# Half of k's features by wide VectorE operations at the start of an attention-and-mixer kernel

## The chip, the core and the metric

The kernel runs on one core of a Trainium2 chip. Its time is device time in microseconds (us), the median of several runs; lower is better. The core has a matrix engine (TensorE, PE in the profile), a vector engine (VectorE, DVE), a scalar engine (ScalarE, ACT), a general engine (GpSimd, POOL) and a queue engine (SyncE, SP) that issues most transfers. Each engine works through its own instructions in the order in which the program gave them; semaphores tie the engines together. The matrix engine writes its sums to PSUM; everything else here lies in SBUF, and inputs and output lie in device memory (HBM).

## What is computed

There are 8 batches, 8 heads, 576 positions and 64 features per head, all inputs float32.

```python
# linear attention with two position-weighted features of relu(q) and relu(k)
theta = pi/2 * pos / S
phi(x) = concat(relu(x) * cos(theta), relu(x) * sin(theta))     # 64 -> 128
kv  = sum over positions of phi(k)^T v          # 128 x 64 per head
z   = sum over positions of phi(k)
x   = (phi(q) kv) / (phi(q) z + 1e-6)           # heads side by side: 576 x 512
# mixer
u   = x + low-rank mix of x over positions (U: 576x32, V: 32x576)
out = u + relu(u @ w_ch1) @ w_ch2               # 512 -> 2048 -> 512
```

## The kernel before

**The bulk.** The mixer's two large products (`g1_main`, line 487, and `g2_part`, line 539) are 1,024 matrix instructions of 128x512, and they are the matrix engine's steady work. Batches go in pairs. The order of all work is written out by hand: a list of slots (one slot is one `g1_main` or a quarter of a `g2` row), and a table `todo` of what is emitted beside each slot. For batches 2 to 7 the attention of a batch is spread over the slots of the pair before it (`attention_plan`). For batches 0 and 1 there is no earlier work to hide behind: batch 0 is worked through by `chain0` before the first slot, and batch 1 is prepared beside slots 0 to 6 (`beside`, lines 754 to 766) and finished by `chain1` after slot 7.

**Batch 0.** Its chain is: load q, k and v; make phi(q) (`q_prep`), transpose it on the matrix engine (`qtr_unit`) and copy the result out of PSUM; make phi(k) (`k_prep`) and a bf16 copy of v with a column of ones (`v_prep`, tile `v_ext`); multiply the two (`kv_unit`); denominators (`den_unit`); x (`xh_unit`); and then the mixer's low-rank step down to the transposed u (`uT`), from which `g1_main` reads. k and v lie as four groups `g` of two heads, each with nine chunks `c` of 64 values per partition. `chain0` goes through the heads in two halves, groups 0 and 1, then groups 2 and 3.

**phi(k).** `k_prep(b, c, engs, g0, g1)` makes one chunk: one instruction for the cosine feature and one for the sine feature, each max(k, 0) times a per-partition weight (a [128, 1] column, since one chunk of one partition is one position). The pair `engs` names the engines. In batch 0's first half the cosine is on VectorE and the sine on ScalarE but for chunks 4 and 8; in its second half VectorE takes the cosine of four chunks and GpSimd that of five (line 659). GpSimd also makes `v_ext` of groups 2 and 3 (lines 661 and 662), after its five chunks. In batch 1 VectorE makes nine cosine chunks of 256 values and ScalarE nine sine chunks (line 760).

**Other pieces the change touches.** `V_four` spreads the small matrix V over PSUM and `V_evac` copies it to SBUF as `V_bf`, between the q transposes and phi(k). `keep_warm(n, tag, bufs)` issues n matrix instructions on zeros whose results nobody reads. SyncE's queue carries, in order: q, k and v of batch 0 in halves, with the tail of q (positions 512 to 575, tile `qt`) between them; then batch 1's q, k, tail of q, and v (lines 731 to 738). A tile with a single buffer can only be loaded when its last reader is done: the tail of q of batch 1 waits for `q_prep(0, 4, ...)`, and v of batch 1 for the four `v_prep` of batch 0. GpSimd issues the loads of `w_ch1` and `w_ch2` (tile `w_bf`), among its casts. The second quarter of `w_ch1` (`w1_load(1)`) comes right after `v_ext` of groups 2 and 3.

Of the kernel before, what the change touches and what calls it, by code (L numbers as in the profile page):

```python
# [13 lines left out]
ALU = mybir.AluOpType  # L14
# [3 lines left out]
def kernel(  # L18
# [11 lines left out]
    nc = tc.nc  # L30

    B = 8
    H = 8
    S = 576
    D = 64
    E = D + 1
    P = 128
# [13 lines left out]
    def tail(b):  # L51
        lo = TS * (b % 2)
        return slice(lo, lo + TS)
# [8 lines left out]
    kst, vst, qst, qt = {}, {}, {}, {}  # L62

    def alloc_k(b):
        kst[b] = pool.tile([P, 4, 9, D], FP32, tag="kst", bufs=2, name="kst")
# [4 lines left out]
    def load_nine(dst, src, b, g0=0, g1=4, eng=None):  # L70
        (eng or nc.sync).dma_start(
            out=dst[:, g0:g1, :, :].rearrange("p g c d -> p g (c d)"),
            in_=src[b].rearrange("(g hh) (p c) d -> (hh p) g (c d)", hh=2, c=9)[:, g0:g1, :],
        )
# [11 lines left out]
    def load_tail(dst, src, b, h0=0, h1=H, eng=None):  # L86
        (eng or nc.sync).dma_start(
            out=dst[tail(b), h0:h1, :],
            in_=src[b, h0:h1, 512:S, :].rearrange("h s d -> s h d"),
        )  # L90
# [4 lines left out]
    def w1_load(n):  # L95
        cs = slice(n * 512, n * 512 + 512)
        nc.gpsimd.dma_start(
            out=w1_bf[:, :, cs], in_=moe_w_ch1.rearrange("(d p) n -> p d n", p=P)[:, :, cs]
        )
# [7 lines left out]
    def cast(eng, o, i):  # L107
        if eng is nc.scalar:
            nc.scalar.activation(out=o, in_=i, func=AF.Copy, bias=0.0, scale=1.0)
        else:  # L110
            eng.tensor_copy(out=o, in_=i)  # L111


    V_, A_, G_ = nc.vector, nc.scalar, nc.gpsimd
# [6 lines left out]
        out=iota[:, 0:4], pattern=[[1, 4]], base=0, channel_multiplier=4,  # L121
        allow_small_or_imprecise_dtypes=True,
    )
    for lo in (0, TS):
        nc.gpsimd.iota(
            out=iota[lo : lo + TS, 4:5], pattern=[[1, 1]], base=512, channel_multiplier=1,
# [3 lines left out]
            out=iota[lo : lo + TS, 5:14], pattern=[[1, 9]], base=0, channel_multiplier=9,  # L130
# [13 lines left out]
    cosw = const.tile([P, 14], FP32)  # L144
    sinw = const.tile([P, 14], FP32)
# [21 lines left out]
        out=U_bf[:, 0:4, :], in_=moe_U[0:512, :].rearrange("(p c) r -> p c r", c=4)  # L167
# [12 lines left out]
    def keep_warm(n, tag, bufs):  # L180
        w_ps = ps.tile([P, 512], FP32, tag=tag, bufs=bufs, name="w_ps")
        for _ in range(n):
            nc.tensor.matmul(out=w_ps, lhsT=zero[:, 0:P], rhs=zero, start=True, stop=True)
# [6 lines left out]
    def V_four(tag, bufs):  # L190
        v4 = v4_ps[0] = ps.tile([P, 2, 512], FP32, tag=tag, bufs=bufs, name="v4_ps")
        lhs = four.rearrange("r g s -> r (g s)")
        nc.tensor.matmul(
            out=v4[:, 0, :].rearrange("m (c p) -> m c p", c=4), lhsT=lhs,
            rhs=V_32[:, 0:512].rearrange("r (p c) -> r c p", c=4), start=True, stop=True,
        )
        for i in range(2):
            nc.tensor.matmul(
                out=v4[:, 1, tail(i)], lhsT=lhs, rhs=V_32[:, 512:S], start=True, stop=True
            )  # L200

    def V_evac(eng):
        cast(
            eng, V_bf.rearrange("p c t -> p (c t)"),
            v4_ps[0].rearrange("p a n -> p (a n)")[:, 0 : 5 * P],
        )


    k_p, q_p, q_pT, kv_sb, x_bf, A_sb = {}, {}, {}, {}, {}, {}
    u_bf, u_tl, uT, uT_tl = {}, {}, {}, {}  # L210

    def v_prep(b, g, eng):
        cast(eng, v_ext[b % 2][:, g, :, 0:D], vst[b][:, g, :, :])
# [9 lines left out]
    def k_prep(b, c, engs, g0=0, g1=4):  # L223
        if b not in k_p:
            k_p[b] = pool.tile([P, 9, 4, 2 * D], BF16, tag="k_p", bufs=1, name="k_p")
        for i, (w, eng) in enumerate(zip((cosw, sinw), engs)):
            if eng is not None:
                scaled_relu(
                    eng, k_p[b][:, c, g0:g1, i * D : i * D + D], kst[b][:, g0:g1, c, :],
                    w[:, 5 + c : 6 + c],  # L230
                )

    def q_prep(b, c, engs, h0=0, h1=H):
        if b not in q_p:
# [10 lines left out]
    def kv_unit(b, g0=0, g1=4, eng=None):  # L245

        if b not in kv_sb:
            kv_sb[b] = pool.tile([P, H, E], BF16, tag="kv", bufs=2, name="kv")
        acc = ps.tile([P, 2, 512], FP32, tag="X", bufs=1, name="kv_ps")
        for g in range(g0, g1):  # L250
            for c in range(9):
                for hh in range(2):
                    rows = slice(hh * TS, hh * TS + TS)
                    nc.tensor.matmul(  # L254
                        out=acc[:, hh, (g - g0) * E : (g - g0) * E + E],
                        lhsT=k_p[b][rows, c, g, :],
                        rhs=v_ext[b % 2][rows, g, c, :],
                        start=(c == 0),
                        stop=(c == 8),
                    )  # L260
        cast(
            eng or V_,
            kv_sb[b][:, 2 * g0 : 2 * g1, :].rearrange("p (g hh) e -> p hh g e", hh=2),
            acc[:, :, 0 : (g1 - g0) * E].rearrange("p hh (g e) -> p hh g e", e=E),
        )
# [5 lines left out]
    def qtr_unit(b, c, h0=0, h1=H, eng=None, tag="T", bufs=1):  # L271
        qT_alloc(b)
        t_ps = ps.tile([P, H, P], BF16, tag=tag, bufs=bufs, name="t_ps")
        for h in range(h0, h1):
            nc.tensor.transpose(  # L275
                out=t_ps[:, h, :],
                in_=q_p[b][:, c, h, :] if c < 4 else q_tl[:, h, :],
                identity=ident,
            )
        if c < 4:  # L280
            cast(eng or V_, q_pT[b][:, c, h0:h1, :], t_ps[:, h0:h1, :])
        else:
            cast(eng or V_, q_tlT[:, h0:h1, tail(b)], t_ps[:, h0:h1, tail(b)])
# [14 lines left out]
    def qT_of(b, c, h):  # L298
        return q_pT[b][:, c, h, :] if c < 4 else q_tlT[:, h, :]
# [12 lines left out]
    def den_unit(b, h0, h1, tag, bufs):  # L312
        n = h1 - h0
        d_ps = ps.tile([P, 5, n], FP32, tag=tag, bufs=bufs, name="d_ps")
        for c in range(5):
            for h in range(h0, h1):
                nc.tensor.matmul(
                    out=d_ps[:, c, h - h0 : h - h0 + 1],
                    lhsT=qT_of(b, c, h),
                    rhs=kv_sb[b][:, h, D:E],  # L320
                    start=True,
                    stop=True,
                )
        rec = pool.tile([P, 5, n], FP32, tag="rec5", bufs=2, name="rec5")
        recip(rec, d_ps)
        return rec
# [312 lines left out]
    O2, G3 = ("o", 2), ("g", 3)  # L639
# [9 lines left out]
        uTd_open(b, 3, "o", 2)  # L649

    def chain0():
        v_prep(0, 0, V_)
        v_prep(0, 1, A_)
        q_prep(0, 4, (V_, A_))
        kv_unit(0, 0, 2)
        keep_warm(2, "o", 2)
        qtr_unit(0, 4, 0, H, V_, *G3)
        for c in range(9):
            k_prep(0, c, (V_ if c < 4 else G_, A_), 2, 4)
        rec0 = den_unit(0, 0, 4, "T", 1)  # L660
        for g in (2, 3):
            v_prep(0, g, G_)
        w1_load(1)
        for n, c in enumerate(TL):
            xh_unit(0, c, 0, 4, rec0, *(O2, O2, G3, G3, G3)[n], A_ if n == 1 else None)
        keep_warm(2, "T", 1)
        kv_unit(0, 2, 4, A_)
        rec1 = den_unit(0, 4, 8, "X", 1)
        a0 = A_unit(0, "T", 1, A_, 0, 256)
        for n, c in enumerate(TL[:3]):  # L670
            xh_unit(0, c, 4, 8, rec1, *(O2, O2, G3)[n])
        chain_begin(0)
        uTd_mm(0, 0)
        uTd_mm(0, 1)
        for n, c in enumerate(TL[3:]):
            xh_unit(0, c, 4, 8, rec1, *G3)
        uTd_evac(0, 0, A_)
        uTd_evac(0, 1, A_)
        keep_warm(2, "o", 2)
        return a0  # L680
# [35 lines left out]
        for c in TL[:4]:  # L716
            q_prep(0, c, (V_, V_ if c == 3 else A_), h, h + 4)
    for c in TL[:4]:
        qtr_unit(0, c, 0, H, (V_, A_, V_, A_)[c], *(G3 if c < 3 else O2))
        if c in (1, 3):  # L720
            keep_warm(1, "X", 1)
    V_four("X", 1)
    V_evac(V_)
    for c in range(9):
        k_prep(0, c, (V_, V_ if c in (4, 8) else A_), 0, 2)
    keep_warm(11, "o", 2)

    G_.tensor_copy(out=mark, in_=vst[0][0:TS, 0, 0, 0:1])
# [2 lines left out]
    alloc_q(1)  # L731
    load_main(qst[1], q, 1)
    alloc_k(1)
    load_nine(kst[1], k, 1)
    load_tail(qt[1], q, 1)
    alloc_v(1)
    load_nine(vst[1], v, 1, 0, 2)
    load_nine(vst[1], v, 1, 2, 4)
# [12 lines left out]
    def at(j, *thunks):  # L751
        beside.setdefault(j, []).extend(thunks)
# [4 lines left out]
        tg = ("T", 1) if n % 2 else O2  # L757
        at(1 + n, lambda c=c, tg=tg: qtr_unit(1, c, eng=V_, tag=tg[0], bufs=tg[1]))
    for c in range(9):
        at(4 + c // 3, lambda c=c: k_prep(1, c, (V_, A_)))  # L760
    at(2, lambda: G_.tensor_copy(out=mark, in_=q_tlT[0:TS, 0, TS : TS + 1]))
    at(2, lambda: [w1_load(2), w1_load(3)])
    at(2, lambda: [v_prep(1, g, G_) for g in (0, 1)])
# [12 lines left out]
    for pr in range(NPAIR):  # L776
        e, o = 2 * pr, 2 * pr + 1
# [57 lines left out]
```

## Time and profile before

| what | value |
|---|---|
| median of 6 runs | 323.76 us (322.81 to 324.41) |
| the profiled execution's own time | 324.41 us |
| its span (first to last record) | 322.1 us |
| PE busy | 310.6 us, 96% of the span |
| VectorE busy | 157.3 us, 49% |
| ScalarE busy | 152.6 us, 47% |
| GpSimd busy | 39.1 us, 12% |
| PE's share of the chain that ended last | 82% |
| transfers' share of that chain | 7% |

The span is one execution; 2.3 us of its time lie outside the span. A busy matrix engine is not one at its peak: its records include the waiting of pipelined instructions on each other, and the `keep_warm` instructions count as busy. So the table says that there is little idle time on the matrix engine over the whole, not where the start of the kernel is held up. That is read from the chain of work that ended last and from the timeline of the first 40 us.

### The profile page before, as it was taken

Reading aid. Unit: us, or ns where it says so; the run is one execution under the profiler, and the core shown is the slowest. Engines: PE = TensorE matmul, PEld = TensorE weight load, DVE = VectorE, ACT = ScalarE, POOL = GpSimd, SP = SyncE. Lnnn points to the kernel's source line nnn. Section 1 sums busy time; section 2 is a strip of 40 time slices with the busy share of each in tenths; the row PEclk is TensorE's granted clock in tenths of the full one; section 3 lists DMA queues with packets and bytes.
Section 4 is the critical chain, followed back from the end, with each engine's and each line's share of the span. In section 5 each row is a group of like instructions: output and inputs, shape, how many; then the busy total and the mean of one; then the engine's idle time right before and its main releaser. Section 6 shows DMA issues by size and latency. Waiting matters only on the chain.

```text
span 322.1 us, 6314 instructions
## 1 busy us (share of the span) xinstructions
PE 310.6 (96%) x2607; PEld 163.2 (51%) x2634; DVE 157.3 (49%) x386; ACT 152.6 (47%) x281; POOL 39.1 (12%) x72
## 2 busy tenths in 40 slices
PE   8779999999999999999999999999999999999995
PEld 4455555476545544466455444565454444464443
DVE  6757763781787646026935586154826520001211
ACT  5836855595905356758400077568300066750000
POOL 4342500300110130000320100000121100000000
PEclk9979999999999999999999999999999999999999
DMA  7996999928099937990799659920592140001131
GB/s 242 330 285 168 179 200 353 361 72 293 35 203 145 290 108 141 240 284 0 136 255 305 221 117 160 342 87 20 119 206 80 62 105 0 2 0 67 65 95 68
DMA packets 67149, 51.85 MB, mean 161 GB/s; under 512 B 43602, under 2 KB 56178, under 8 KB 67122
## 3 DMA queue, kind: packets, MB, share of 16 engines
q1 hardware_dynamic: 60194, 40.05, 47.6%
q0 software_dynamic: 6784, 11.35, 15.2%
q8 instruction: 20, 0.33, 0.4%
q10 hardware_dynamic: 144, 0.07, 0.1%
q14 instruction: 7, 0.06, 0.0%
HBM read 36.86 MB, written 9.44 MB: 144 GB/s over the span
## 4 chain that ended last, share of the span: by engine, by line
PE 82%; DMA 7%; DVE 4%; ACT 3%; issue 1%; SPq 1%; POOL 1%; DVEq 0%; POOLq 0%
PE o_ps L539 36%; PE g_ps L487 31%; DMA qt<-in_q_dram 4%; PE gt_ps L507 4%; DMA kst<-in_k_dram 3%; PE kv_ps L254 3%; PE x_ps L359 2%; PE va_ps L403 2%; ACT hid L496 1%; DVE k_p L219 1%; ACT k_p L217 1%; PE a_ps L386 1%; DVE u_bf L404 1%; ACT q_p L217 1%; PE t_ps L275 1%
## 5 line engine op out<-in xcount | busy, mean ns | idle before, releaser
L496 ACT ACTIVATE hid<-g_ps 128x512 bf16<-128x512 f32 x128 | 76.2, 596 | 102.7 <-PE g_ps L487 102.6
L487 PE MATMUL g_ps<-uT,w_bf 128*128 128x512 bf16 x512 | 118.2, 379 | 0.2
L539 PE MATMUL o_ps<-w_bf,hid 128*128 128x512 bf16 (+2 forms) x510 | 117.0, 372 | 1.1 <-issue 0.2
L487 PEld LDWEIGHTS <-w_bf 128*128 128x128 bf16 x512 | 48.9, 98 | 56.4 <-issue 0.4
L539 PEld LDWEIGHTS <-hid 128*128 128x128 bf16 x528 | 48.8, 98 | 53.8 <-issue 2.0
L549 DVE TENSOR_TENSOR o_sb<-u_bf,o_ps 128x512 f32<-128x512 bf16 (+2 forms) x33 | 22.0, 668 | 62.4 <-PE o_ps L539 62.3
L559 POOL DMA_DIRECT2D out_dram<-o_sb x24 | 14.7, 611 | 166.1 <-DVE o_sb L549 156.7
L404 DVE TENSOR_TENSOR u_bf<-x_bf,va_ps 128x512 bf16<-128x512 bf16 x32 | 21.7, 684 | 10.6 <-PE va_ps L403 9.8
L219 DVE TENSOR_SCALAR k_p<-kst,cosw 128x256 bf16<-128x256 f32 (+1 forms) x63 | 20.4, 351 | 0.0
L111 DVE CAST kv<-kv_ps 128x520 bf16<-128x520 f32 (+1 forms) x8 | 5.1, 632 | 28.9 <-PE kv_ps L254 28.9
L217 ACT ACTIVATE k_p<-kst,sinw 128x256 bf16<-128x256 f32 (+1 forms) x43 | 17.2, 455 | 0.5 <-DMA kst<-in_k_dram 0.5
L369 DVE TENSOR_TENSOR x_bf<-x_ps,rec 128x512 bf16<-128x512 f32 x24 | 16.6, 691 | 0.8
L217 ACT ACTIVATE q_p<-qst,sinw 128x512 bf16<-128x512 f32 (+1 forms) x24 | 15.1, 658 | 2.3 <-DMA qst<-in_q_dram 2.2
L309 DVE TENSOR_SCALAR rec<-x_ps 128x8 f32<-128x8 f32 (+1 forms) x30 | 5.0, 165 | 22.1 <-PE x_ps L359 22.0
L507 PE MATMUL gt_ps<-uT_tl,w_bf 128*128 128x128 bf16 x256 | 15.6, 219 | 0.0
L539 PE MATMUL o_ps<-w_bf,hid_tl 128*128 128x512 bf16 x62 | 14.7, 379 | 0.2 <-issue 0.2
L507 PEld LDWEIGHTS <-w_bf 128*128 128x128 bf16 x256 | 14.6, 98 | 0.5
L254 PE MATMUL kv_ps<-v_ext,k_p 64*128 64x65 bf16 x576 | 12.0, 191 | 2.7 <-DVE v_ext L111 1.5
L254 PEld LDWEIGHTS <-k_p 64*128 64x128 bf16 x576 | 10.7, 94 | 6.7 <-issue 3.8
L403 PE MATMUL va_ps<-A_sb,V_bf 128*128 128x512 bf16 x37 | 14.0, 379 | 0.0
L219 DVE TENSOR_SCALAR q_p<-qst,cosw 128x512 bf16<-128x512 f32 (+1 forms) x28 | 12.3, 460 | 1.7 <-DMA qst<-in_q_dram 1.6
L219 DVE TENSOR_SCALAR k_p<-kst,sinw 128x256 bf16<-128x256 f32 (+1 forms) x38 | 13.0, 342 | 0.0
(97 smaller groups left out, 230.7 us busy)
## 6 DMA issues: line engine op xcount, KB each, us to landing
kst<-in_k_dram SPq DMA_DIRECT2D x7, 1152.0 KB, 9.6
qst<-in_q_dram SPq DMA_DIRECT2D x7, 1024.0 KB, 13.6
vst<-in_v_dram SPq DMA_DIRECT2D x6, 1152.0 KB, 9.6
out_dram<-o_sb POOLq DMA_DIRECT2D x24, 256.0 KB, 4.2
w_bf<-in_moe_w_ch_dram POOLq DMA_DIRECT2D x8, 512.0 KB, 11.3
vst<-in_v_dram SPq DMA_DIRECT2D x4, 576.0 KB, 10.7
out_dram<-o_sb SPq DMA_DIRECT2D x7, 256.0 KB, 2.3
kst<-in_k_dram SPq DMA_DIRECT2D x2, 576.0 KB, 9.1
```

The source lines that it names most:

```text
L217: nc.scalar.activation(out=o, in_=i, func=AF.Relu, bias=0.0, scale=w)
L219: eng.tensor_scalar(out=o, in0=i, scalar1=0.0, scalar2=w, op0=ALU.max, op1=ALU.mult)
L254: nc.tensor.matmul(out=acc[:, hh, (g - g0) * E : (g - g0) * E + E], lhsT=k_p[b][rows, c, g, :], rhs=v_ext[b % 2][rows, g, c, :], start=(c ...
L369: nc.vector.tensor_tensor(out=x_of(b, c, rows).rearrange("p (g i d) -> p g i d", g=2, d=D), in0=view[:, :, :, 0:D], in1=rec[rows].unsqueez ...
L403: nc.tensor.matmul(out=va, lhsT=V_bf[:, c, :], rhs=A_sb[b], start=True, stop=True)
L404: nc.vector.tensor_tensor(out=u_bf[b][:, c, :] if c < 4 else u_tl[b // 2][rows, :], in0=x_of(b, c, rows), in1=va[rows, :], op=ALU.add,)
L487: nc.tensor.matmul(out=g_ps.rearrange("p (c t) -> p c t", c=4), lhsT=w1_bf[:, d, j * P : j * P + P], rhs=uT[b][:, :, d, :], start=(d == 0) ...
L496: nc.scalar.activation(out=hid[b][:, j, :], in_=g_ps, func=AF.Relu, bias=0.0, scale=1.0)
L507: nc.tensor.matmul(out=g_ps[:, jj, :], lhsT=w1_bf[:, d, j * P : j * P + P], rhs=uT_tl[pr][:, d, :], start=(d == 0), stop=(d == 3),)
L539: nc.tensor.matmul(out=o[:, cols], lhsT=lhs[:, j, c * P : c * P + P], rhs=w2_bf[:, j, cols], start=(j == 0), stop=(j == NJ - 1),)
L549: nc.vector.tensor_tensor(out=o_sb[:, cols], in0=u[:, cols], in1=o[:, cols], op=ALU.add)
L559: eng.dma_start(out=out[b, 0:512, cols].rearrange("(p c) n -> p c n", c=4)[:, c, :], in_=o_sb[:, cols],)
```

## The change

A new function `k_wide(b, i, c0, c1, g0, g1)` makes one feature (0 is cosine, 1 is sine) of the chunks c0 to c1 of a group in one VectorE instruction per group: `scalar_tensor_tensor`, max with 0, then times a tensor of weights, which is the weight columns spread over 64 values. In batches 0 and 1 it takes the cosine of all nine chunks, a group at a time (576 values), and in batch 0's first half also the sine of chunks 6 to 8. ScalarE keeps the other sine chunks. GpSimd makes no chunk of k any more; it starts with `v_ext` of groups 2 and 3. `V_four` and `V_evac` move between the q transposes of chunk 1 and chunk 2, and the copy goes from VectorE to ScalarE; the copy of chunk 3's transposes goes from ScalarE to VectorE. `v_prep(0, 1)` is emitted before `v_prep(0, 0)` (they are on different engines). In the second half of batch 0 the two wide operations stand before and after `den_unit`. Some `keep_warm` calls change place and number: after the q transposes there is one after each chunk instead of two in all, one instead of two stands after the first `kv_unit`, and a new one after the second. On SyncE's queue the tail of q of batch 1 moves ahead of k of batch 1.

```diff
+    def k_wide(b, i, c0, c1, g0, g1):
+        w = (cosw, sinw)[i][:, 5 + c0 : 5 + c1].unsqueeze(2).to_broadcast([P, c1 - c0, D])
+        for g in range(g0, g1):
+            nc.vector.scalar_tensor_tensor(
+                out=k_p[b][:, c0:c1, g, i * D : i * D + D], in0=kst[b][:, g, c0:c1, :],
+                scalar=0.0, in1=w, op0=ALU.max, op1=ALU.mult,
+            )
...
     def chain0():
+        v_prep(0, 1, A_)
         v_prep(0, 0, V_)
-        v_prep(0, 1, A_)
         q_prep(0, 4, (V_, A_))
         kv_unit(0, 0, 2)
-        keep_warm(2, "o", 2)
+        keep_warm(1, "o", 2)
         qtr_unit(0, 4, 0, H, V_, *G3)
-        for c in range(9):
-            k_prep(0, c, (V_ if c < 4 else G_, A_), 2, 4)
-        rec0 = den_unit(0, 0, 4, "T", 1)
         for g in (2, 3):
             v_prep(0, g, G_)
         w1_load(1)
+        for c in range(9):
+            k_prep(0, c, (None, A_), 2, 4)
+        k_wide(0, 0, 0, 9, 2, 3)
+        rec0 = den_unit(0, 0, 4, "T", 1)
+        k_wide(0, 0, 0, 9, 3, 4)
         for n, c in enumerate(TL):
             xh_unit(0, c, 0, 4, rec0, *(O2, O2, G3, G3, G3)[n], A_ if n == 1 else None)
         keep_warm(2, "T", 1)
         kv_unit(0, 2, 4, A_)
+        keep_warm(1, "T", 1)
         rec1 = den_unit(0, 4, 8, "X", 1)
...
     for c in TL[:4]:
-        qtr_unit(0, c, 0, H, (V_, A_, V_, A_)[c], *(G3 if c < 3 else O2))
-        if c in (1, 3):
-            keep_warm(1, "X", 1)
-    V_four("X", 1)
-    V_evac(V_)
-    for c in range(9):
-        k_prep(0, c, (V_, V_ if c in (4, 8) else A_), 0, 2)
+        qtr_unit(0, c, 0, H, (V_, A_, V_, V_)[c], *(G3 if c < 3 else O2))
+        if c == 1:
+            V_four("X", 1)
+            V_evac(A_)
+        keep_warm(1, "o", 2)
+    for c in range(6):
+        k_prep(0, c, (None, A_), 0, 2)
+    k_wide(0, 0, 0, 9, 0, 2)
+    k_wide(0, 1, 6, 9, 0, 2)
     keep_warm(11, "o", 2)
...
     load_main(qst[1], q, 1)
     alloc_k(1)
+    load_tail(qt[1], q, 1)
     load_nine(kst[1], k, 1)
-    load_tail(qt[1], q, 1)
     alloc_v(1)
...
     for c in range(9):
-        at(4 + c // 3, lambda c=c: k_prep(1, c, (V_, A_)))
+        at(4 + c // 3, lambda c=c: k_prep(1, c, (None, A_)))
+    for n, g in enumerate((0, 2)):
+        at(4 + n, lambda g=g: k_wide(1, 0, 0, 9, g, g + 2))
```

## The prediction

> **What bounds the kernel now.** I read the chain of work that ended last first. From 37.5 us on it is almost only the matrix engine: what is saved there can only be an earlier start. The pieces ahead of that, in order of time (start, length, what):
>
> ```profile
> 14.09 13.74 DMA qt<-in_q_dram
> 27.82 0.03 issue
> 27.85 0.49 DVE q_tl L219
> ...
> 34.60 1.20 ACT k_p L217 x3
> 35.79 0.48 ACT hid L496
> 36.27 1.20 ACT k_p L217 x3
> ...
> 37.52 0.52 PE kv_ps L254 x20
> ```
>
> The matrix engine's first multiply of batch 1 ends a ScalarE run, and that run begins when the tail of batch 1's q lands at 27.8. The same stretch by engine (busy time of PE, weight loads, DVE, ACT, POOL) shows two engines with no slack:
>
> ```profile
> 27.85:37.50 9.65, 8.86 (x81) 5.50 (x80) 9.12 (x21) 9.27 (x20) 6.11 (x9) 1.00 0.75 129
> ```
>
> So the time is "when can ScalarE and VectorE start on batch 1", plus 9.65 us, plus fixed matrix work. Two things set the start: the landing of the tail, and the end of batch 0's chain. SyncE's queue in the timeline says why the landing is late:
>
> ```profile
> 7.52 0.37 SPq L81 DMA_DIRECT2D qst<-in_q_dram  x1
> 7.93 3.60 SPq L71 DMA_DIRECT2D kst<-in_k_dram  x1
> 14.09 0.62 SPq L87 DMA_DIRECT2D qt<-in_q_dram  x1
> ```
>
> 128 KB stand behind q's 1024 KB (landed 7.52 + 13.7 = 21.2) and k's 1152 KB (7.93 + 17.2 = 25.1). And batch 0's chain, from the timelines of VectorE, GpSimd, PE and ScalarE:
>
> ```profile
> 9.81 0.82 DVE L111 CAST V_bf<-v_ps 128x640 bf16<-128x640 f32 x1 [0.90 <-PE v_ps L198]
> 12.89 0.73 DVE L111 CAST v_ext<-vst 128x576 bf16<-128x576 f32 x1
> ...
> 14.23 3.52 POOL L219 TENSOR_SCALAR k_p<-kst,cosw 128x128 bf16<-128x128 f32 x5 [1.35 <-DMA kst<-in_k_dram]
> 17.71 1.28 POOL L111 CAST v_ext<-vst 128x576 bf16<-128x576 f32 x2
> ...
> 19.04 0.47 PE L254 MATMUL kv_ps<-v_ext,k_p 64*128 64x65 bf16 x18 [0.15 <-POOL v_ext L111]
> ...
> 26.41 0.60 ACT L109 ACTIVATE uT<-uT_ps 128x512 bf16<-128x512 f32 x1 [1.64 <-PE uT_ps L452]
> ```
>
> The second `kv_unit` waits for GpSimd. The chain ends with uT at 27.0; ScalarE then sits 0.85 us for the tail. In the window view the matrix clock is halved in a part of this chain (the column before DMA share):
>
> ```profile
> 20.35:23.76 3.41, 3.19 (x45) 2.43 (x43) 1.54 (x5) 0.47 (x2) 0.00 (x0) 0.51 1.14 271
> ```
>
> **What the Trainium skill says.** "VectorE: DVE Perf Modes", the perf-mode tier table: fp32 tensor by scalar runs two elements a cycle, tensor by tensor one. The trace agrees: 128x256 against 128x512 tensor_scalars start 0.285 and 0.40 us apart (0.45 ns an element), the 128x512 tensor_tensor x_bf took 0.691 us. The wide form has a second tensor, so I price it as a tensor_tensor; the page doesn't list it. "SBUF — State Buffer", who interferes with whom: a VectorE operation with two SBUF inputs and a GpSimd operation that reads SBUF block one another whole. The trace shows the like: VectorE's 128x128 chunks took up to 0.514 us beside GpSimd's at 15.9 to 17.1, 0.277 at best. "TensorE: Matmul & The Clock Gate", part 1: free-running windows of 3.413 us, and an idle one halves the clock. The slow stretch here is 3.41 us, after a window with gaps at 16.8 to 18.4 and 19.5 to 20.0.
>
> **Price of the wide operation.** 576 values by the x_bf row: 0.691 + 64/0.96 = 0.76 us; next start after 0.67 (x_bf 128x256: three in 1.09, one 0.42, so 0.335 apart, of which 0.267 is elements; 0.6 + 0.07). Bounds: 0.40 if it ran two a cycle, 1.27 if one element took two cycles. I take 0.67.
>
> **First half of batch 0.** V lands at 9.05 (2.15 + 6.9) in both. Before, PE had all transposes done by then; now chunks 2 and 3 stand behind `V_four` (ends 9.77). They are ready at about 10.4 and 11.05. VectorE: two copies of 0.65 from 10.4 to 11.7; two wide cosines, 1.34; two sines of 192 values at 0.27 (0.145 + 192 x 0.52 ns, fitted to 0.21 at 128 and 0.285 at 256), 0.54; v_ext 0.73: ends 14.3, against 13.62. So the first kv starts at 14.5 instead of 13.77: 0.7 later. ScalarE copies V at 9.8 (0.71, between its 0.60 for 512 and 1.02 for 1024 bf16), then six sines, v_ext and tail: free at 13.7, before k's second half lands at 14.05, so its later work doesn't move.
>
> **Second half.** GpSimd loses 3.52 us of k. v's second half lands at 15.5 (4.31 + 11.2): its two casts run 15.5 to 16.8, and `w1_load(1)` is issued at 16.9 instead of 18.94. VectorE: kv copied by 15.7, tail transposes copied by 16.45 (a `keep_warm` less buys 0.2), wide g2 at 16.4, or at 16.8 if it waits for GpSimd's cast; I take 16.8, to 17.5; rec 17.5 to 18.0; wide g3 to 18.7; x copies to 20.0, 1.0 later than the 19.0 of before. The second kv: g3 at 18.8 to 19.2; ScalarE's copy to 19.7; denominators at 19.7 instead of 19.99. So the chain gains only 0.3 here: GpSimd's wait goes, VectorE's takes its place. But PE does xh, two `keep_warm`, 36 kv, one more `keep_warm` and the denominators between 16.9 and 20.3 without a gap of over 0.5: some 1.9 us of streaming against about 1.1. I expect no halved window; that saves 1.2 us (12 xh, 13 matrix instructions of `a_ps` and `u`, at 3.41 us for what takes 2.2).
>
> **Sum to the start of batch 1.** 27.0 - 0.3 - 1.2 = 25.5 for uT. The first quarter of w1 is a floor: it landed at 23.8 (12.09 + 11.7), and uT ended 1.7 after g1 began (25.3 to 27.0), so 25.5 too; if GpSimd's `mark` copy waits for a wide operation at 11.8, up to 26.1. The tail of q now stands behind q alone: issued at 14.8 (its buffer is freed by VectorE's q_tl at 14.75), it lands at about 22: covered by 3 us. ScalarE starts at 25.5 to 26.1 instead of 27.85: 1.75 to 2.35 gained.
>
> **What moves with the queue.** k of batch 1 is issued at 15.4 instead of 7.93. Transfers don't run dry: by 15 us some 4.4 MB of 5.8 MB issued have moved at 300 GB/s, so k starts when q is done, as before, 0.13 MB later: about 25.5. Needed: 32.82 - 2.2 = 30.6. v of batch 1 behind it, 29 to 30.6 as now; its casts are needed at 34. The second quarter of w1 goes 2 us earlier, lands at about 28.6, and is needed at 31.26 - 2.2 = 29.1: half a microsecond of cover; without it PE and then ScalarE wait.
>
> **Batch 1's stretch.** VectorE's nine chunks (33.41 to 37.0, with one copy: 3.07 without) become four wide ones, 2.7: -0.4, but ScalarE's nine sines are unchanged and end the stretch at 37.47. I count nothing; without that cover it would be -0.4. All later stages are the same and PE-bound, so the earlier start carries to the end.
>
> **Total.** 2.1 off (the middle of 1.75 to 2.35): the profiled execution's 324.41 (span 322.1) would be 322.3. The median, 323.76, is 0.65 better than that execution, and if a faster transfer made it so, part of that is already what I count. I halve it: 322.0.
>
> **Rivals.** (1) The clock still halves, or VectorE's 0.7 in the first half is not recovered: uT at 26.7 to 27.3, the tail no longer waited for: 0.5 to 1.2 gained, 322.6 to 323.3. For it: the window's phase is free, and VectorE carries more. Against it: the denser PE. (2) k of batch 1 is the new late transfer: with its 17.2 us to landing from 15.4 it comes at 32.6, and ScalarE's first sine is back at 32.6 against 32.82: 323.5, no change. Against: k of another batch, issued at 45.1, landed in 8.1. (3) Slower: the wide form costs two cycles an element, 1.27 apart. Four of them stand in batch 0's chain (+2.4: uT at 27.9, the gain gone), and four in batch 1's stretch, where VectorE would have 9.12 - 3.07 + 5.08 = 11.1 us of work in 9.65: +1.5, so 325.3. It decides from about d = 1.08, where 2.35 = 4(d - 0.67) + 4(d - 0.90). For it: no row of this form, four strided dimensions. Against: x_bf has a broadcast operand too. (4) More than forecast: no GpSimd block, w1 early, VectorE's 0.4 counts: 320.6 to 321.4.
>
> **Chances.** Forecast 0.55 (321.6 to 322.4), rival 1 0.20, rival 2 0.05, rival 3 0.08, rival 4 0.12. A measurement can tell about 0.3%, 1.0 us: below 322.8 is faster, above 324.7 slower. Forecast and rival 4 are faster, 0.67, and a third of rival 1, 0.07: 0.74. Rival 3 is slower: 0.08. The rest, 0.18, is no change. The range leaves out the lower half of rival 4 (0.06), rival 3 (0.08) and rival 2's upper end: 320.9 to 323.5.
>
> **What would show it.** The tail of q no longer ends a wait on ScalarE; uT's last copy ends near 25.5 to 26; the first kv starts near 14.5; GpSimd's v_ext near 15.5; wide operations of 0.76 us; clock 1.00 from 20 to 24; w1's second quarter landed by 29. Wrong if wide operations take over 1 us, if g1 at slot 4 waits for w1 or k_p for k, or if a halved window falls elsewhere in the chain.

## The result

The changed kernel takes 322.05 us (median of 13 runs, 320.08 to 323.53). The kernel before, measured again beside it, takes 324.92 us (28 runs, 322.81 to 326.23). The ratio is 0.9911, with a 95% interval of 0.9888 to 0.9934: 2.9 us, or 0.9%, faster. The forecast was 322.0. The profiled execution took 321.07 us with a span of 318.7, against 324.41 and 322.1 before.

The chain of work that ended last, for the changed kernel (start, length, what):

```profile
2.14 5.78 DMA V<-in_moe_V_dram
...
13.38 0.75 PE kv_ps L263 x36
...
23.88 1.73 PE g_ps L496 x8
25.61 0.45 PE t_ps L284 x8
...
33.09 1.20 ACT k_p L217 x3
...
34.34 0.51 PE kv_ps L263 x20
```

The tail of q is gone from the chain; the chain now goes back to the landing of V. Batch 1's first multiply still ends with ScalarE's sines, but starts its last 20 instructions at 34.3 instead of 37.5. SyncE's queue, from the timeline:

```profile
7.50 0.37 SPq L81 DMA_DIRECT2D qst<-in_q_dram  x1
13.78 0.62 SPq L87 DMA_DIRECT2D qt<-in_q_dram  x1
14.44 0.63 SPq L71 DMA_DIRECT2D kst<-in_k_dram  x1
```

The tail, issued at 13.78, lands 7.8 us later, at 21.6. Batch 0's chain in the timeline (start, length, engine, what, idle time before it and its releaser):

```profile
9.44 1.35 DVE L111 COPY q_pT<-t_ps 128x1024 bf16<-128x1024 bf16 x2 [1.41 <-PE t_ps L284]
10.71 1.42 DVE L237 SCALAR_TENSOR_TENSOR k_p<-kst,cosw 128x576 bf16<-128x576 f32 x2
...
14.28 1.28 POOL L111 CAST v_ext<-vst 128x576 bf16<-128x576 f32 x2 [2.89 <-DMA vst<-in_v_dram]
...
15.51 0.76 POOL L97 DMA_DIRECT2D w_bf<-in_moe_w_ch_dram  x1
...
16.83 0.86 PE L263 MATMUL kv_ps<-v_ext,k_p 64*128 64x65 bf16 x36
...
23.92 0.60 ACT L109 ACTIVATE uT<-uT_ps 128x512 bf16<-128x512 f32 x1 [1.56 <-PE uT_ps L461]
...
24.54 0.72 ACT L217 ACTIVATE q_tl<-qt,sinw 64x512 bf16<-64x512 f32 x1
```

uT ends at 24.5 and ScalarE goes on to batch 1 at once; before it ended at 27.0 and waited until 27.85. And the stretch of batch 1 by engine (PE, weight loads, DVE, ACT, POOL, clock, share and GB/s of transfers):

```profile
24.54:34.33 9.79, 9.21 (x84) 5.34 (x83) 8.36 (x16) 9.29 (x20) 5.99 (x9) 1.00 1.12 260
```

It is as long as before (9.79 against 9.65); VectorE is busy 0.8 us less in it, ScalarE the same. Not all of the 3.4 us between the two spans is the change: in this execution the same early transfers also landed 1.1 to 1.3 us sooner than in the one profiled before (k's second half at 12.7 against 14.05, v's at 14.2 against 15.5, V 1.1 sooner), though nothing ahead of them was changed. The medians carry the comparison.

k of batch 1, now issued behind the tail at 14.44, landed 12.4 us later, at 26.8; ScalarE's first sine on it starts at 29.6. So the prediction's second rival, k as the new late transfer, falls.

### The profile page after: what moved, and what is told of

The parts are those of the page before. It is cut to its first block, busy times and chain, and to the rows that moved or that the text cites. A ratio compares the mean times of both kernels' runs of the same rounds, so it can differ in the third digit from the quotient of the medians.

```text
span 318.7 us, 6289 instructions
## 1 busy us (share of the span) xinstructions
PE 308.8 (97%) x2609; PEld 161.6 (51%) x2636; DVE 156.4 (49%) x372; ACT 151.5 (48%) x280; POOL 35.3 (11%) x67
## 4 chain that ended last, share of the span: by engine, by line
PE 87%; DVE 4%; ACT 4%; DMA 2%; issue 2%; POOL 0%; POOLq 0%; DVEq 0%
PE o_ps L548 37%; PE g_ps L496 33%; PE gt_ps L516 4%; PE kv_ps L263 3%; PE x_ps L368 3%; PE va_ps L412 2%; DMA V<-in_moe_V_dram 2%; PE t_ps L284 1%; PE a_ps L395 1%; ACT hid L505 1%; DVE k_p L219 1%; ACT k_p L217 1%; PE xh_ps L343 1%; DVE u_bf L413 1%; ACT q_p L217 1%
## 5 line engine op out<-in xcount | busy, mean ns | idle before, releaser
L219 DVE TENSOR_SCALAR k_p<-kst,cosw 128x256 bf16<-128x256 f32 x41 | 13.9, 345 | 0.0
L219 DVE TENSOR_SCALAR q_p<-qst,cosw 128x512 bf16<-128x512 f32 (+1 forms) x28 | 11.7, 441 | 1.7 <-DMA qst<-in_q_dram 1.6
L219 DVE TENSOR_SCALAR k_p<-kst,sinw 128x256 bf16<-128x256 f32 x36 | 12.3, 343 | 0.0
```

The source lines that it names most:

```text
L219: eng.tensor_scalar(out=o, in0=i, scalar1=0.0, scalar2=w, op0=ALU.max, op1=ALU.mult)
```

## The experiments

Each run is given by its ratio to the kernel before on the same chip; the changed kernel's is 0.9911 (0.9888 to 0.9934). Intervals are 95%. The kernel before was measured in five sessions, with medians from 324.17 to 324.92 us. The changed kernel was measured in one of them only, and each ratio is uncertain by about 0.2% or more, so ratios that lie closer together are not told apart here.

### The tail of q alone

The kernel before, with this edit:

```diff
+    load_tail(qt[1], q, 1)
     load_nine(kst[1], k, 1)
-    load_tail(qt[1], q, 1)
```

> The kernel before with one edit: the tail of q of batch 1 is issued ahead of k. Theory A (two late things stand one behind the other: uT at 27.0, then the tail at 27.85; the tail is the last): the wait for the tail on ScalarE goes, uT is the new end, so batch 1 starts at 27.0 instead of 27.85 in an execution like the profiled one; 0.3 to 0.9 us faster, more (up to 2) where the clock is not halved in batch 0's chain. Theory B (the transfer was hidden and only GpSimd's chunks mattered): no change, within 0.2 us. Theory C (the whole gain is the queue's order): all of it, 2.5 us or more.

Measured: 323.03 us, ratio 0.9967 (0.9948 to 0.9986): 1.1 us faster. From the timeline of this run:

```profile
18.27 0.82 POOL L97 DMA_DIRECT2D w_bf<-in_moe_w_ch_dram  x1
...
24.95 0.72 ACT L217 ACTIVATE q_tl<-qt,sinw 64x512 bf16<-64x512 f32 x1
...
29.89 1.04 PE L487 MATMUL g_ps<-uT,w_bf 128*128 128x512 bf16 x4 [1.23 <-DMA w_bf<-in_moe_w_ch_dram]
```

The direction is theory A's, but the trace shows something that no theory had: batch 1 now starts at 24.95, about as early as in the changed kernel (the clock was not halved in this execution's chain), and then the matrix engine stands 1.23 us at slot 4 for the second quarter of w1. GpSimd issued it at 18.27, behind its five chunks of k and two casts. So GpSimd's chunks cost time by delaying a transfer. That became theory W of the next runs; theory K is the prediction's own sum, in which they cost time through the second kv.

### GpSimd's chunks put back

The changed kernel, batch 0's second half as before:

```diff
+        for c in range(9):
+            k_prep(0, c, (V_ if c < 4 else G_, A_), 2, 4)
+        rec0 = den_unit(0, 0, 4, "T", 1)
         for g in (2, 3):
             v_prep(0, g, G_)
         w1_load(1)
-        for c in range(9):
-            k_prep(0, c, (None, A_), 2, 4)
-        k_wide(0, 0, 0, 9, 2, 3)
-        rec0 = den_unit(0, 0, 4, "T", 1)
-        k_wide(0, 0, 0, 9, 3, 4)
```

> The changed kernel with batch 0's second half as before: VectorE four and GpSimd five narrow cosine chunks, then GpSimd's two casts of v, then the second quarter of w1. Theory W (from the trace of the tail moved alone, where the matrix engine waited 1.23 us for that quarter of w1 at slot 4: GpSimd's chunks cost time by delaying the issue of w1, not by holding the second kv): w1 is issued at about 18 and lands at about 30; uT at about 25 to 25.5; matrix engine idle about 1 us at slot 4 with w1 as the releaser; 0.8 to 1.6 us slower than the changed kernel. Theory K (my prediction's sum: the chain through the second kv is what gains): uT 0.3 us later, or 1.5 with a halved clock window, and no wait for w1.

Measured: 322.41 us, ratio 0.9945 (0.9922 to 0.9969), some 1.1 us worse than the changed kernel by the ratios. The two intervals overlap, so it is the trace that decides. Two lines of its timeline, and its waits (who waited for whom, us in total, times, longest):

```profile
17.83 0.82 POOL L97 DMA_DIRECT2D w_bf<-in_moe_w_ch_dram  x1
...
24.16 0.60 ACT L109 ACTIVATE uT<-uT_ps 128x512 bf16<-128x512 f32 x1 [1.57 <-PE uT_ps L461]
```

```profile
PEld L496 <- DMA w_bf<-in_moe_w_ch_dram: 1.6, 1, 1.6
PE g_ps L496 <- DMA w_bf<-in_moe_w_ch_dram: 1.4, 1, 1.4
```

The second quarter of w1 was issued at 17.83 and landed 12.0 later, at 29.8. uT ended at 24.76, only 0.24 later than in the changed kernel's trace. The first kv, which lies ahead of the edit, already started 0.24 later (13.62 against 13.38), so the chain itself lost next to nothing. Theory W holds.

### Two transfers moved, nothing else

The kernel before, with the tail ahead of k (the edit shown above) and the second quarter of w1 ahead of GpSimd's chunks:

```diff
+        w1_load(1)
         for c in range(9):
             k_prep(0, c, (V_ if c < 4 else G_, A_), 2, 4)
         rec0 = den_unit(0, 0, 4, "T", 1)
         for g in (2, 3):
             v_prep(0, g, G_)
-        w1_load(1)
```

> The kernel before with two edits on transfers alone: the tail of q of batch 1 ahead of k, and the second quarter of w1 issued ahead of GpSimd's chunks (at about 12.8 instead of 18.3). Theory W: no wait for w1 at slot 4, and the whole gain of the change or nearly so, 2.0 to 2.9 us faster than before, without any wide operation. Theory K: about as the tail alone, 1.1 us faster.

Measured: 322.72 us, ratio 0.9950 (0.9930 to 0.9971): 1.6 us, between the two forecasts. From its timeline:

```profile
11.34 1.56 POOL L97 DMA_DIRECT2D w_bf<-in_moe_w_ch_dram  x2
...
24.56 0.72 ACT L217 ACTIVATE q_tl<-qt,sinw 64x512 bf16<-64x512 f32 x1
...
28.10 1.03 PE L487 MATMUL g_ps<-uT,w_bf 128*128 128x512 bf16 x4
```

Batch 1 starts at 24.56, slot 4 runs at 28.10 without a wait for w1, and the span is 319.7. But the 22 times spread from 321.2 to 325.5, twice as wide as with GpSimd's chunks put back into the changed kernel (322.05 to 324.09). The mean granted clock of each execution (the share of full speed that the matrix engine was given) parts them without overlap: ten with 0.998 or more took 321.2 to 322.3 us, twelve with 0.995 or less took 322.7 to 325.5. Whether the clock was the cause or a late transfer brought both, this run alone doesn't say; the next two runs change the instructions on zeros.

### The clock: instructions on zeros taken away, and put in

First, the changed kernel without four of them:

```diff
         kv_unit(0, 0, 2)
-        keep_warm(1, "o", 2)
...
-        keep_warm(2, "T", 1)
         kv_unit(0, 2, 4, A_)
-        keep_warm(1, "T", 1)
```

> The changed kernel without the four instructions on zeros that stand in batch 0's chain after the first kv, ahead of the second and behind it. My step says that the window of the matrix clock stays full because the matrix engine streams more between 17 and 20, these four among it: without them a halved window of 3.41 us in the chain, uT 0.5 to 1.2 us later, time 0.4 to 1.2 us higher. Rival: the clock is kept by the rest, and four instructions less are 0.2 us saved.

Measured: 322.41 us, ratio 0.9941 (0.9918 to 0.9963), about 1 us worse than the changed kernel by the ratios (the intervals overlap), and the 22 times spread from 320.7 to 324.5. Two stretches of its profile in the window view, where the clock stands before the transfers' share, then the end of its chain:

```profile
13.65:17.06 3.41, 2.74 (x87) 2.44 (x80) 2.88 (x8) 3.41 (x13) 1.95 (x2) 1.00 1.15 305
17.06:23.89 6.83, 6.03 (x81) 3.74 (x81) 3.35 (x11) 1.90 (x5) 0.97 (x2) 0.54 1.14 297
...
25.62 0.60 ACT L109 ACTIVATE uT<-uT_ps 128x512 bf16<-128x512 f32 x1 [2.43 <-PE uT_ps L461]
```

The second stretch in the changed kernel:

```profile
17.06:23.89 6.83, 6.00 (x109) 3.73 (x103) 4.43 (x14) 2.39 (x7) 0.00 (x0) 1.00 1.15 263
```

The clock is halved from about 17.6 to 24.4, that is for two windows or 6.83 us (the 0.54 is a mean with the first half microsecond still at full clock). uT ends at 26.2, 1.7 us later than in the changed kernel's trace, where the clock is not halved in the chain. But v's second half also landed 0.8 later in this execution, and 0.2 of the 1.7 is there already when the denominators behind the second kv begin (18.40 against 18.18). So the trace alone doesn't separate the missing instructions from the late v. The count of executions does: without the four instructions 2 of 22 had a mean clock of 0.998 or more, with them 9 of 14 (the 13 runs and the profiled execution).

Second, the kernel with the two moved transfers, with more of them:

```diff
-        keep_warm(2, "T", 1)
+        keep_warm(5, "T", 1)
         kv_unit(0, 2, 4, A_)
+        keep_warm(1, "T", 1)
```

> The kernel before with the two transfers moved (tail of q ahead of k, second quarter of w1 ahead of GpSimd's chunks) and four more instructions on zeros in batch 0's chain: five instead of two ahead of the second kv, one behind it. No wide operation, V's copy where it was. If the change works through these three things alone (transfers and clock), the times have one cluster near 321.0 to 321.8, no halved window in the chain, and the kernel is 2.5 to 3.2 us faster than before, as the changed kernel or better. If the wide operations and V's place bring something of their own on top, it stays 0.5 us or more behind the changed kernel.

Measured: 321.84 us, ratio 0.9916 (0.9898 to 0.9934), with times from 321.49 to 322.43 and no halved window. GpSimd's five chunks and its casts still hold the second kv in this run:

```profile
13.53 3.77 POOL L219 TENSOR_SCALAR k_p<-kst,cosw 128x128 bf16<-128x128 f32 x5
17.25 1.27 POOL L111 CAST v_ext<-vst 128x576 bf16<-128x576 f32 x2
...
24.53 0.60 ACT L109 ACTIVATE uT<-uT_ps 128x512 bf16<-128x512 f32 x1 [1.56 <-PE uT_ps L452]
25.04 0.49 DVE L219 TENSOR_SCALAR q_tl<-qt,cosw 64x512 bf16<-64x512 f32 x1
25.15 0.72 ACT L217 ACTIVATE q_tl<-qt,sinw 64x512 bf16<-64x512 f32 x1
```

So without a single wide operation, and with V's copy where it was, two moved transfers and four instructions on zeros give 0.9916; the change as a whole gave 0.9911. By the ratios, what the wide form adds of its own is below what these runs can tell.

A sharper reading takes only the executions at full clock, here those with a mean of 0.998 or more (as an estimate, one halved window of 3.41 us in 322 takes 0.005 off the mean; the kernel before, profiled with one, had 0.995), and compares their spans:

| kernel | executions at full clock | median span of these, us |
|---|---|---|
| before, in four sessions | 22 of 137 | 322.0 |
| before, tail moved | 13 of 22 | 320.9 |
| before, tail and w1 moved | 10 of 22 | 319.7 |
| the same, four more instructions on zeros | 6 of 6 | 319.9 |
| changed | 9 of 14 | 319.3 |
| changed, GpSimd's chunks put back | 9 of 12 | 320.5 |
| changed, without four instructions on zeros | 2 of 22 | 319.0 |

With the clock set aside, the two transfers bring 2.3 of the 2.7 us, and the instructions on zeros bring nothing that shows but the clock. The remaining 0.4 to 0.6 us may belong to the wide operations, to V's place or to a difference between sessions; no run isolates it.

### The tail put back

The changed kernel with the tail behind k again (the first diff, reversed):

> The changed kernel with one edit: the tail of q of batch 1 goes back behind k. Theory A: batch 0's chain still ends at about 24.5 to 25.5, but ScalarE and VectorE then wait for the tail until 26.5 to 27.8; 2 to 2.9 us of the gain are lost against the changed kernel, so within 0.8 us of the kernel before. Theory B: no loss. Theory C: the whole gain is lost too, so this run alone doesn't part A from C; the first run does.

Measured: 323.69 us, ratio 0.9980 (0.9962 to 0.9999): nearly four fifths of the gain lost. Its profile can't be read for the tail, since V came late in that execution and the chain with it:

```profile
10.22 0.61 PE L193 MATMUL v_ps<-V,four 32*128 32x512 bf16 x1 [2.27 <-DMA V<-in_moe_V_dram]
...
17.39 0.76 PE L263 MATMUL kv_ps<-v_ext,k_p 64*128 64x65 bf16 x36 [0.77 <-DVE v_ext L111]
```

uT ended at 27.96 there, and the tail had landed at 27.8. The matrix clock was halved for one window of this chain, not for two as the next expectation says. A second run put the tail back in the combined kernel described below, whose chain doesn't hang on V:

> The combined kernel (early w1, V behind the q transposes, more instructions on zeros) with the tail of q of batch 1 back behind k. The first run with the tail put back was profiled in an execution where V came late and the clock halved twice, so its chain was late too and the tail's own cost could not be read. Here the chain no longer hangs on V: theory A: uT ends at 23.8 to 25.2, ScalarE then stands idle with the tail as the releaser until it lands at 26 to 27.8; 1.5 to 3 us slower than the combined kernel (320.9), so 322.4 to 323.9. Theory B (the tail's place is worth nothing once w1 and the clock are mended): no change against the combined kernel.

Measured: 324.44 us, ratio 0.9998 (0.9980 to 1.0015): the whole gain of the combined kernel is gone, more than expected. From its timeline:

```profile
24.48 0.60 ACT L109 ACTIVATE uT<-uT_ps 128x512 bf16<-128x512 f32 x1 [2.82 <-PE uT_ps L461]
27.22 0.72 ACT L217 ACTIVATE q_tl<-qt,sinw 64x512 bf16<-64x512 f32 x1 [2.15 <-DMA qt<-in_q_dram]
```

The chain is done at 25.1, and ScalarE waits 2.15 us for the tail. It would have been done sooner still: the matrix engine had waited 1.08 us for the first quarter of w1, which the prediction named as a floor, and that wait too is hidden behind the tail. An earlier chain is worth nothing while the tail is behind k. This is theory A, shown.

### V behind the q transposes

```diff
-        if c == 1:
-            V_four("X", 1)
-            V_evac(A_)
         keep_warm(1, "o", 2)
+    V_four("X", 1)
+    V_evac(A_)
```

> The changed kernel with V's spreading and its copy (still on ScalarE) placed behind all four q transposes instead of between the second and the third. My step says that the transposes of chunks 2 and 3 stand behind V's landing and that this puts VectorE's first half 0.7 us back: if so, VectorE's copies of chunks 2 and 3 run from about 8.2 to 9.6 without waiting for V, the first kv starts 0.7 to 1.0 us earlier than in the changed kernel, and the time is 0.3 to 1.0 us lower. Rival: the second half is held by ScalarE's nine sines and by the landing of k's and v's second halves, so an earlier first half is given back: no change, within 0.2 us.

Measured: 321.64 us (8 runs), ratio 0.9901 (0.9868 to 0.9935), not told apart from the changed kernel's. From its timeline:

```profile
12.49 0.89 PE L263 MATMUL kv_ps<-v_ext,k_p 64*128 64x65 bf16 x36 [0.21 <-DVE v_ext L111]
...
14.94 2.01 POOL L111 CAST v_ext<-vst 128x576 bf16<-128x576 f32 x2 [2.39 <-DMA vst<-in_v_dram]
...
17.00 0.46 PE L263 MATMUL kv_ps<-v_ext,k_p 64*128 64x65 bf16 x18 [0.59 <-POOL v_ext L111]
```

The first kv starts at 12.5 with V's spreading at 9.1; in the changed kernel it started at 13.4 with V 1.2 us sooner. So the step is real, about 2 us at equal landing. But most is given back at the second kv, which waits for v's second half and GpSimd's casts of it, and in this execution the clock was halved once in the chain and once after it.

### Batch 1's cosines narrow again

```diff
-        at(4 + c // 3, lambda c=c: k_prep(1, c, (None, A_)))
-    for n, g in enumerate((0, 2)):
-        at(4 + n, lambda g=g: k_wide(1, 0, 0, 9, g, g + 2))
+        at(4 + c // 3, lambda c=c: k_prep(1, c, (V_, A_)))
```

> The changed kernel with batch 1's cosines back in nine narrow operations of 256 values on VectorE. I counted nothing for the wide form there, since ScalarE's nine sines end the stretch: no change, within 0.3 us. Rival: VectorE is the bound with 9.1 of 9.65 us busy, and the narrow form costs its 0.4 us: 0.3 to 0.5 slower.

Measured: 322.45 us, ratio 0.9934 (0.9910 to 0.9957), which overlaps the changed kernel's. In its trace the second quarter of w1 was late by 0.60 us, so neither the median nor the trace isolates the form of the cosines. The ratios differ by 0.2%, and the spans at full clock by 0.2 us (319.5 in ten executions against 319.3), which fits the forecast of next to no change. The times of these executions lie further apart (322.4 against 321.1 by their medians), mostly outside the span, so this stays open.

### Further steps: w1 early, more zeros, V behind q

The changed kernel with `w1_load(1)` ahead of GpSimd's two casts:

> The changed kernel with the second quarter of w1 issued ahead of GpSimd's two casts instead of behind them (about 12 instead of 15.5 to 17). Theory W: its cover was thin (in the trace with batch 1's narrow chunks slot 4 waited 0.6 us for it), so 0 to 0.6 us faster than the changed kernel. Rival: it takes bandwidth from k and v of batch 1, which come later by the same bytes, and ScalarE waits for k: 0 to 1 us slower.

Measured: 320.79 us (6 runs), ratio 0.9893 (0.9859 to 0.9927). With one instruction on zeros more on either side of the second kv, and four instead of two ahead of batch 1's:

> The changed kernel with the second quarter of w1 issued early, one more instruction on zeros ahead of the second kv, one more behind it, and four instead of two ahead of batch 1's first kv. If halved windows make the slower half of the changed kernel's times, its times (320.1 to 323.5) become narrower at their lower end: median 320.3 to 320.9. If the early w1 alone did that, no difference to that run (320.79).

Measured: 320.94 us, ratio 0.9900 (0.9878 to 0.9922): no difference to the one before it. And with V behind the q transposes on top:

> The former kernel and V's spreading behind all four q transposes. Where V lands late, VectorE's first half no longer waits for it (the first kv at about 12.5 instead of 13.4 to 14.5, up to 17.4 in the worst trace); the second half is held by the landing of v's second half and GpSimd's two casts, so most of it is given back: 0 to 0.6 us faster than the former, with fewer slow runs.

Measured: 320.92 us, ratio 0.9889 (0.9869 to 0.9910), span 318.2. All three have a median about 1 us below the changed kernel's 322.05, but the intervals overlap with its own, so only "as fast or faster" is shown. Of their 18 executions 17 kept the full clock.

## Why the prediction was right

**The order of the two late things** was right. The tail moved alone brought a gain, and put back it took most of the gain away, or all of it. That the first was 1.1 us, near the 0.85 that I read off the profiled execution, is chance: in its trace the start of batch 1 moved by 2.9 (27.85 to 24.95), and 1.23 went back into the wait for w1.

**GpSimd's relief** had the wrong route. I let it work through the second kv and allowed the chain 0.3 us for it; put back, its chunks cost the chain 0.24 at most. That part was about right, but small. I priced the earlier second quarter of w1 only as a cover that must not fail: half a microsecond, which is what the changed kernel's trace has (landed at 27.6, used at 28.08). I did not see that this cover is what the relief is worth: once batch 1 starts at 25, a w1 issued at 18 is 1.2 to 1.4 us late. In the kernel before it was issued and used at

```profile
18.94 0.82 POOL L97 DMA_DIRECT2D w_bf<-in_moe_w_ch_dram  x1
...
31.26 1.03 PE L487 MATMUL g_ps<-uT,w_bf 128*128 128x512 bf16 x4
```

It landed at 30.64 (11.7 us after its issue), 0.6 ahead of its use, and so left no mark in the waits.

**The clock step** was right in kind: the changed kernel keeps the full clock more often, and taking four instructions on zeros away brings the halved windows back, some 1.5 us on uT for two windows, where I had 1.2 for one. It is not kept always: five of the 14 executions fell to 0.993 or less, with a median of 323.5 us, so the first rival came true in a third of them. The Trainium skill, "TensorE: Matmul & The Clock Gate", part 1, has the window's length; every halved stretch seen here in the first 45 us is 3.41 us or twice that. What I had not said is that this term was worth little in the kernel before, whose tail landed after the halved chain was done: there the executions below full clock have a median span only 0.6 us longer, against 1.6 with the two transfers moved.

**The first half** was right: wide operations of 0.75 us (0.76 forecast) next to one another by 0.67, and VectorE later because the transposes of chunks 2 and 3 stand behind V. At equal landing of V the loss is what I gave: V 1.15 us sooner, first kv 0.4 sooner, so 0.7 to 0.75 back. The third rival, two cycles an element, falls.

**The wait on GpSimd's port**, which the Trainium skill, "SBUF — State Buffer", who interferes with whom, made me add as 0.4 us, was smaller in the changed kernel's trace: the wide operation beside GpSimd's cast took 0.886 us against 0.75. It varies with how the two meet: with batch 1's narrow cosines the same operation took 1.24.

**Size.** I took 2.1 off the profiled execution and then halved the median's distance from it, to 1.8; measured by the ratio it is 2.9. The term that was too small is the start of batch 1: the sum had 1.75 to 2.35, and the traces show 3.3 (27.85 to 24.54), of which up to about 1.2 may be the sooner landing of transfers in that execution. The halving was the other part: the kernel before, run 28 times, has a median of 324.92 and not 323.76, so its profiled execution, at 324.41, was not slower than usual. A base 1.2 us too low and a gain 1.1 too small nearly cancel. That the forecast met 322.05 so closely is therefore mostly luck; that the kernel became faster, and through the tail, is not.

## What to carry to other kernels

When a wait is removed, ask of each transfer that the same engine issues later when it will now be needed and when it is issued: a transfer that lands 0.6 us ahead of its use is the next bound and doesn't show in the waits. An engine that computes and also issues transfers delays the transfers by its computing (the second quarter of w1 went out at 18.3, and at about 12 when it stood ahead of the chunks); moving one issue ahead of the computing can bring what moving the computing to another engine brings. And two late things that stand one behind the other must be changed together: here the tail alone brought 1.1 of 2.9 us, and everything but the tail about 0.6 in one kernel and nothing in another.

## What was not expected

V's place makes the start of the kernel depend on one small transfer of 36 KB, through both VectorE's copies and ScalarE's. In the run with the tail put back V landed about 2 us later than in the changed kernel's trace, and the first kv started 4 us later (17.39 against 13.38): the matrix engine stood idle for V, and the window after that ran at half the clock. From the window view of that run:

```profile
7.50:10.14 2.64, 0.45 (x8) 0.27 (x5) 0.56 (x1) 1.02 (x1) 0.00 (x0) 1.00 1.16 308
10.14:13.56 3.42, 3.34 (x22) 2.37 (x23) 0.69 (x1) 2.59 (x8) 0.92 (x2) 0.55 1.05 329
```

Also, wide operations and GpSimd's casts do stretch one another where they meet. In the run with batch 1's narrow cosines the first wide operation of batch 0's second half took 1.24 us beside the casts, against 0.75 alone; in the run with V behind the transposes the two casts took 0.86 and 1.19 us instead of about 0.65.
